# First rows of `a` by a broadcast transfer, block 0's carries ahead of the gate, and the last block's output in a tile for each sequence on two queues

## The chip, the cores and the metric

The kernel runs on one core of one Trainium2 chip. The metric is the device time of one execution in microseconds (us). Of repeated runs the median is quoted. A run is compared with runs of the kernel before on the same chip in the same rounds. On trace times: "at 23.67" is a time in us from the start of the profiled span, which is 1.7 to 1.8 us shorter than the device time.

## The reference

Two blocks in a row: a chunked state-space scan over 4 sequences of 768 steps with 8 heads, then an FFN over the 3072 tokens with a gate `h * cos(h)`. Cut to what matters:

```python
def _attn_ref(x, a, B, C):            # x (4,8,768,32), a (4,8,768), B and C (4,8,768,16)
    log_a = np.log(np.clip(a, 1e-06, 1.0))
    for c in range(nc):
        L = np.exp(cum[..., :, None] - cum[..., None, :]) * causal
        y[:, :, sl] = einsum(CB * L, xc) + einsum(Cc, state) * exp(cum)
        state = decay_full * state + sum(B_j x_j decay_from_j)

def _moe_ref(x, w_in, w_out):         # x (3072,256), w_in (256,2048), w_out (2048,256)
    h = x @ w_in
    return (h * np.cos(h)) @ w_out
```

The weights come as 8-byte floats and are turned into 4-byte ones on the chip, piece by piece.

## The kernel before

It works in 6 blocks of 128 steps for all 4 sequences (512 tokens). Block 0's scan runs alone; from then on, the FFN of block c (16 steps f: a product `hp`, a gate, a product `o`) is interleaved with the scan of block c + 1. TensorE carries nearly everything.

Block 0's decay rows: the row of each head has to stand in all 128 partitions. TensorE makes it by a product with a column of the identity, eight instructions for four heads:

```python
    def spread_a(b, tags):
        u, b_ = b // (NB // NU), b % (NB // NU)
        spread[b] = []
        for t in range(2):
            a_ps = bank([P, HH, P], "a_ps", tags[t])
            for h in range(HH):
                r = (b_ * H + t * HH + h) * NC
                PE.matmul(a_ps[:, h], lhsT=ident[0:RB, r:r + 1].to_broadcast([RB, P]),
                          rhs=cut[:, u], start=(h == 0), stop=True, skip_group_check=True)
            spread[b].append(a_ps)
```

A scan on the vector engine (DVE) turns each half into `lam`. Then transposes (`tp`), ScalarE's copies (`cT`, `bcT`), products `g`, DVE's `m`, products `y`, and the first FFN product. All transfers are issued by one queue, SyncE's (SP), in this order: `a`, then B, C, x of each sequence of block 0, six weight pieces, `a` back to DRAM, then for block 1:

```python
    load(1)                # B, C and x of all sequences, in pieces of 64, 64 and 128 bytes
    load_along(1)
    for b in range(NB):
        load_a(1, (b,))    # sequence b's decay rows, "arow"
        for n in (6 + 2 * b, 7 + 2 * b):
            fetch(*order[n])   # weight pieces
```

The main loop:

```python
    for n in range(NC * NF + LAG):
        c, f = divmod(n, NF)
        ...
            first(n)                                   # hp, k (ScalarE), w (DVE)
            if n + 3 < len(order):
                rest = grade(*order[n + 3], later=True)  # ScalarE, GpSimd: a weight piece
            if n + 2 < len(order):
                join(*order[n + 2])                    # DVE, GpSimd: the piece before it
            gate(n)                                    # sine (ScalarE), gT (DVE)
        if n >= LAG:
            second(n - LAG)                            # o
        if n < NB:
            carry(0, n)                                # s_ps (TensorE), state (DVE)
        if c + 1 < NC:
            ...   # (turn, intra, finish) of block c + 1: a sequence in three steps, from f = 3 on
```

At the end, four copies of `o` go into two output tiles, DVE and ScalarE in turn, and four transfers go out on SP's queue. In the last block `o` is a pair of PSUM tiles of two banks each, two sequences to a tile.

## Time and profile before

| | before |
|---|---|
| median of 3 runs | 410.0 us |
| TensorE busy, share of the span | 98% |
| first transpose | 9.22 us |
| first `hp` (f = 0) | 23.67 us |
| `hp` of f = 4 / f = 6 | 36.64 / 45.59 us |
| end of the last matmul / of the span | 404.2 / 408.6 us |

From the timeline of ScalarE: start, duration, engine, line, operation, operands, and in brackets the idle time in front of it and what ended it.

```profile
36.09 0.69 ACT L170 ACTIVATE mag<-words 128x512 f32<-128x512 f32 x1 [0.94 <-DMA words<-in_moe_w_in_dram]
```

ScalarE waits 0.94 us for a weight piece, the seventh asked for, in the middle of block 1's scan. TensorE waits for nothing there.

### The profile page before, as it was taken

How to read it: one execution, taken by the hardware profiler on the slowest of the kernel's cores; microseconds unless marked ns; L12 is line 12 of the kernel's file. 1: busy time of each engine (PE TensorE's matmuls, PEld its weight loads, DVE VectorE, ACT ScalarE, POOL GpSimd, SP SyncE). 2: the span in 40 equal slices, each digit the busy share in tenths (PEclk: the TensorE clock that was granted, in tenths of full speed). 3: DMA queues.
4: the chain of work that ended last, by engine and by line, in shares of the span. 5: the costliest groups of instructions: out<-in, count | busy, mean ns of one | idle time of the engine just before them, and what ended most of it. 6: DMA issues, size and time to landing. Idle time of an engine off the chain costs nothing.

```text
span 408.6 us, 5540 instructions
## 1 busy us (share of the span) xinstructions
PE 401.1 (98%) x2094; PEld 263.1 (64%) x2094; DVE 266.7 (65%) x410; ACT 173.8 (43%) x329; POOL 42.3 (10%) x62
## 2 busy tenths in 40 slices
PE   8999999999999999999999999999999999999995
PEld 6646666666666666666666666666666666666664
DVE  4989999945768754777663677674566664444442
ACT  2476666534343434344334433433434342433332
POOL 2164555400000000000000000000000000000000
PEclk9999999999999999999999999999999999999999
DMA  7999994291111092110164211120100000100001
GB/s 96 327 138 309 390 177 113 62 120 54 51 52 53 0 171 63 53 43 10 51 117 65 70 34 51 53 78 0 53 1 2 0 0 2 51 0 2 0 0 53
DMA packets 105979, 30.28 MB, mean 74 GB/s; under 512 B 75168, under 2 KB 101856, under 8 KB 105952
## 3 DMA queue, kind: packets, MB, share of 16 engines
q1 hardware_dynamic: 105952, 29.92, 30.9%
q8 instruction: 16, 0.26, 0.3%
q14 instruction: 11, 0.09, 0.1%
HBM read 26.57 MB, written 3.34 MB: 73 GB/s over the span
## 4 chain that ended last, share of the span: by engine, by line
PE 97%; ACT 1%; DVE 1%; issue 0%; DVEq 0%
PE hp L361 42%; PE o L385 41%; PE g L302 4%; PE y L324 3%; PE y L320 2%; PE a_ps L251 2%; PE warm L94 1%; PE tp L283 1%; PE tp L284 1%; PE s_ps L341 1%; PE y L94 0%; ACT cT L288 0%; ACT w L372 0%; DVE m L306 0%; DVE gT L374 0%
## 5 line engine op out<-in xcount | busy, mean ns | idle before, releaser
L361 PE MATMUL hp<-yT,w_in 128*128 128x512 f32 x384 | 185.0, 604 | 0.6 <-DVE gT L374 0.6
L385 PEld LDWEIGHTS o<-w_out,gT 128*128 128x128 f32 x768 | 145.9, 190 | 59.9 <-issue 44.0
L385 PE MATMUL o<-w_out,gT 128*128 128x256 f32 x768 | 181.1, 379 | 0.0
L365 ACT ACTIVATE k<-hp 128x512 int32<-128x512 f32 x96 | 57.4, 597 | 127.2 <-PE hp L361 127.1
L374 DVE TENSOR_TENSOR gT<-hp,w 128x512 f32<-128x512 f32 x96 | 66.3, 690 | 65.4 <-ACT w L372 65.4
L367 DVE SCALAR_TENSOR_TENSOR w<-hp,k 128x512 f32<-128x512 f32 x96 | 66.0, 687 | 62.3 <-ACT k L365 60.9
L361 PEld LDWEIGHTS hp<-yT,w_in 128*128 128x128 f32 x384 | 67.8, 190 | 57.7 <-issue 53.7
L372 ACT ACTIVATE w<-w,quarter 128x512 f32<-128x512 f32 x96 | 69.3, 722 | 75.1 <-DVE w L367 75.1
L267 DVE TENSOR_TENSOR_SCAN lam<-arow,unit 128x512 f32<-128x512 f32 x40 | 48.6, 1214 | 0.0
L306 DVE TENSOR_TENSOR m<-g,lam 128x512 f32<-128x512 f32 x48 | 30.7, 681 | 0.7 <-PE g L302 0.6
L276 POOL TENSOR_TENSOR sc<-bc,lam 128x128 f32<-128x128 f32 x20 | 8.2, 412 | 203.0 <-DVE lam L267 200.6
L288 ACT ACTIVATE cT<-tp,slot 128x128 f32<-128x128 f32 x48 | 14.6, 355 | 12.7 <-PE tp L284 12.7
L302 PE MATMUL g<-cT,bcT 32*128 32x256 f32 x192 | 17.1, 426 | 1.2 <-ACT bcT L290 1.2
L324 PE MATMUL y<-m,xr 128*32 128x128 f32 x384 | 15.8, 279 | 0.2 <-DVE m L306 0.2
L191 DVE SCALAR_TENSOR_TENSOR mag<-words,mag 128x512 uint32<-128x512 uint32 x16 | 13.4, 840 | 0.6
L329 ACT COPY yT<-y 128x256 f32<-128x256 f32 x24 | 8.9, 372 | 11.3 <-PE y L324 11.3
L302 PEld LDWEIGHTS g<-cT,bcT 32*128 32x128 f32 x192 | 7.5, 182 | 8.7 <-issue 6.5
L320 PEld LDWEIGHTS y<-bcT,state 128*128 128x128 f32 x80 | 12.1, 191 | 1.0
L171 POOL TENSOR_SCALAR mag<-mag 128x512 f32<-128x512 f32 x16 | 11.7, 731 | 9.4 <-ACT mag L170 9.2
L320 PE MATMUL y<-bcT,state 128*128 128x128 f32 x80 | 12.2, 274 | 0.0
L324 PEld LDWEIGHTS y<-m,xr 128*32 128x32 f32 x384 | 8.9, 109 | 4.3 <-DVE m L306 1.4
L170 ACT ACTIVATE mag<-words 128x512 f32<-128x512 f32 x16 | 10.9, 681 | 0.9 <-DMA words<-in_moe_w_in_dram 0.9
(43 smaller groups left out, 156.0 us busy)
## 6 DMA issues: line engine op xcount, KB each, us to landing
arow<-a_cut SPq DMA_DIRECT2D x20, 512.0 KB
words<-in_moe_w_in_dram SPq DMA_DIRECT2D x8, 512.0 KB
words<-in_moe_w_out_dram SPq DMA_DIRECT2D x8, 512.0 KB
xr<-in_x_dram SPq DMA_DIRECT2D x5, 512.0 KB
out_dram<-ob SPq DMA_DIRECT2D x10, 256.0 KB
bc<-in_B_dram SPq DMA_DIRECT2D x5, 256.0 KB
bc<-in_C_dram SPq DMA_DIRECT2D x5, 256.0 KB
along<-a_all SPq DMA_DIRECT2D x20, 64.0 KB
```

The source lines that it names most:

```text
L267: V.tensor_tensor_scan(out=lam[c, b][:, hs].rearrange("p h i -> p (h i)"), data0=rows_.rearrange("p h i -> p (h i)"), data1=unit.rearrange ...
L288: ACT.activation(cT[:, t], tp[:, 1], AF.Copy, scale=slot[:, t:t + 1])
L302: PE.matmul(g[u // 2][:, u % 2, 0:2 * P], lhsT=bcT[r, 0], rhs=cT[r].rearrange("p t i -> p (t i)"), start=True, stop=True)
L306: V.tensor_tensor(out=m[:, hs].rearrange("p (k t) i -> p k (t i)", k=2), in0=g[u][:, :, 0:2 * P], in1=l[:, hs].rearrange("p (k t) i -> p k ...
L320: PE.matmul(y[:, t], lhsT=s[:, t * P:(t + 1) * P], rhs=bcT[:, 1], start=(t == 0), stop=False, skip_group_check=True)
L324: PE.matmul(y[32 * q:32 * q + 32, t], lhsT=xr[:, b, h], rhs=m[:, h], start=(c == 0 and t == 0), stop=True, tile_position=(0, 32 * q), skip ...
L361: PE.matmul(hp[n], lhsT=w_in[:, k, f * P:(f + 1) * P], rhs=yT[c][:, k], start=(k == 0), stop=(k == KT - 1))
L365: ACT.activation(k, hp[n], AF.Copy, bias=0.25, scale=INV_2PI)
L367: V.scalar_tensor_tensor(out=w, in0=hp[n], scalar=INV_2PI, in1=k, op0=ALU.mult, op1=ALU.subtract)
L372: ACT.activation(cos, cos, AF.Sin, bias=quarter, scale=TWO_PI)
L374: V.tensor_tensor(out=gT[n], in0=hp.pop(n), in1=cos, op=ALU.mult)
L385: PE.matmul(o[c][b // 2][:, b % 2], lhsT=g[:, b * P:(b + 1) * P], rhs=w_out[:, f], start=(f == 0 and (last or b % 2 == 0)), stop=(f == NF ...
```

## The change

Three edits, each to shorten what TensorE or the end waits for: (1) sequence 0's first four heads get their rows by a broadcast transfer of 256 KB on ScalarE's queue, so that eight products fall away; (2) the states of block 0 are made ahead of the gates of n = 0, 1, 2, in DVE's idle time, instead of after the second product; (3) the last output gets a tile for each sequence, and two queues.

```diff
+    row0 = const.tile([P, HH, P], FP32, name="row0")
+    nc.scalar.dma_start(out=row0, in_=a[0, 0:HH, 0:P].unsqueeze(0).to_broadcast([P, HH, P]))
     a_in = const.tile([RB, NU, P], FP32, name="a_in")
 ...
+    V.tensor_scalar(out=row0, in0=row0, scalar1=1.0, scalar2=1e-6, op0=ALU.min, op1=ALU.max)
+    V.memset(row0[:, :, 0:1], 0.0)
 ...
-        spread[b] = []
-        for t in range(2):
+        spread[b] = [] if b else [row0]
+        for t in range(len(spread[b]), 2):
 ...
+        if last:
+            for b in range(NB):
+                ob = two.tile([P, DM], FP32, tag="ob1", bufs=NB, name="ob")
+                (ACT.copy if b == 1 else V.tensor_copy)(out=ob, in_=o[c][b // 2][:, b % 2])
+                (nc.scalar if b % 2 else nc.sync).dma_start(out=rows_[:, b, c, :], in_=ob)
+            return
 ...
+            for b in ((0,), (1, 2), (3,))[n] if n < 3 else ():
+                carry(0, b)
             gate(n)
 ...
-        if n < NB:
-            carry(0, n)
```

More of the change, by code (lines that the diff above doesn't have):

```diff
@@ L390, in second @@
         rows_ = out.rearrange("(b c p) m -> p b c m", b=NB, p=P)
-        count = 1 if last else 2
-        for i in range(0, NB, count):
-            if i % 2 == 0:
-                ob = two.tile([P, 2, DM], FP32, tag="ob", name="ob")
-            bs = slice(i % 2, i % 2 + count)
-            (ACT.copy if (i // count) % 2 else V.tensor_copy)(out=ob[:, bs],
-                                                             in_=o[c][i // 2][:, bs])
-            nc.sync.dma_start(out=rows_[:, i:i + count, c, :], in_=ob[:, bs])
+        if last:
[4 more added lines that the diff above has]
+            return
+        for i in range(2):
+            ob = two.tile([P, 2, DM], FP32, tag="ob", name="ob")
+            (ACT.copy if i else V.tensor_copy)(out=ob, in_=o[c][i])
+            nc.sync.dma_start(out=rows_[:, 2 * i:2 * i + 2, c, :], in_=ob)
     fill(bank([P, 4, P], "warm", "o"), 2)
-    spread_a(0, ("h", "h"))
+    spread_a(0, (None, "h"))
     decays(0, 0, 0)
```

## The prediction

> **What bounds the kernel now.** I read the page first, then the chain that ended last in order of time, then the timeline of the first 33 us and of the last 6 us, since the change touches only these two stretches.
>
> ```profile
> PE 401.1 (98%) x2094; PEld 263.1 (64%) x2094; DVE 266.7 (65%) x410; ACT 173.8 (43%) x329; POOL 42.3 (10%) x62
> ...
> PE 97%; ACT 1%; DVE 1%; issue 0%; DVEq 0%
> ```
>
> TensorE carries 97% of the chain. Between 36 and 403 us nothing of the program changes, so what can be won is time before the first FFN products find their rhythm, and time after the last matmul. The chain, in order of time, shows the beginning:
>
> ```profile
> 1.12 3.78 PE warm L94 x4
> 4.90 4.48 PE a_ps L251 x32
> 9.39 0.11 PE tp L283
> 9.50 0.12 PE tp L284
> 9.62 0.02 issue
> 9.64 0.63 ACT cT L288 x2
> ...
> 27.77 0.70 DVE gT L374
> 28.48 0.14 issue
> 28.61 1.96 PE hp L361 x4
> 30.57 1.73 PE o L385 x8
> 32.29 0.25 PE s_ps L341 x8
> ```
>
> Columns: start, duration, engine, tile, line. To see: 32 a_ps matmuls stand between the warm-up fills and sequence 0's transposes, on TensorE itself; and from 25.64 to 28.61 the chain leaves TensorE (k, w, sine, gT), because the third hp waits for gT to free one of two hp banks. TensorE's wait there is 0.57 us on the timeline ("PE hp L361 <- DVE gT L374: 0.6, 1").
>
> DVE's timeline of the same place:
>
> ```profile
> 26.29 0.69 DVE L367 SCALAR_TENSOR_TENSOR w<-hp,k 128x512 f32<-128x512 f32 x1
> 27.77 0.69 DVE L374 TENSOR_TENSOR gT<-hp,w 128x512 f32<-128x512 f32 x1 [0.79 <-ACT w L372]
> 28.38 0.41 DVE L346 TENSOR_TENSOR state<-s_ps,own 128x256 f32<-128x256 f32 x1
> 28.82 0.69 DVE L367 SCALAR_TENSOR_TENSOR w<-hp,k 128x512 f32<-128x512 f32 x1
> 29.43 0.42 DVE L189 TENSOR_SCALAR mag<-mag 128x512 uint32<-128x512 uint32 x1
> 29.88 0.98 DVE L191 SCALAR_TENSOR_TENSOR mag<-words,mag 128x512 uint32<-128x512 uint32 x1
> 30.78 0.68 DVE L374 TENSOR_TENSOR gT<-hp,w 128x512 f32<-128x512 f32 x1
> ```
>
> DVE has one hole, 0.79 us before gT(0); after it it is full until about 52 us. The end:
>
> ```profile
> 403.35 0.42 DVE L396 COPY ob<-o 128x256 f32<-128x256 f32 x1 [1.46 <-PE o L385]
> 403.80 1.83 SPq L398 DMA_DIRECT2D out_dram<-ob  x4
> 403.81 0.37 ACT L396 COPY ob<-o 128x256 f32<-128x256 f32 x1 [2.64 <-DVE ob L396]
> 404.21 0.42 DVE L396 COPY ob<-o 128x256 f32<-128x256 f32 x1 [0.44 <-PE o L385]
> 404.67 0.37 ACT L396 COPY ob<-o 128x256 f32<-128x256 f32 x1 [0.49 <-DVE ob L396]
> ```
>
> Two copies share a tile, so ACT's copy follows DVE's although it needs other columns. Both DVE copies start only when a pair of sequences is through on TensorE (403.33 and 404.19).
>
> **What the Trainium skill says.** "TensorE: Matmul & The Clock Gate", section "What's actually happening": TensorE starts at half rate, and the warm-up is an amount of busy time, not of matmuls. The trace agrees in kind: the first nine a_ps matmuls start 0.213 us apart, from 6.77 us on they start 0.111 us apart. (It says some 3.4 us; here the fast rate comes 5.5 us after the first fill, and the measurement decides.) So leaving out the first eight a_ps matmuls does not save eight slow ones. "DMA: Bandwidth & Descriptors", section "Issuing engines are not separate DMA queues": DMAs started from different engines run on the same 16 DMA engines and interleave; a second queue saves only issue time. No other issuing queue is in use before, so this trace cannot show it; it does show the 16 engines full from 3 us on (busy share 0.95 to 1.05 in most 2 us stretches from 4 to 24). The same page, "Anatomy of one DMA", gives a fixed cost near 2 us for a DMA from GpSimd, mostly completion. Here, from Sync, a_in issues at 0.81 and lands at 2.58 to 2.95; the last output issues at 405.22 and lands at 407.00 on fifteen engines and at 407.54 on one.
>
> **Part 1, first rows by broadcast.** Removed: the 8 a_ps matmuls of heads 0 to 3. Added: a 256 KB transfer (512 pieces of 512 B) on ACT's queue, a DVE clip over 128x512 (0.42 us, as L189 takes) and a small memset (0.06 us, as the one on quarter). TensorE still starts a_ps at 4.70, after the fills. Eight slow steps end at 6.405 as before, then two of 0.213 and 0.148, then 14 of 0.111: 6.405 + 0.36 + 1.56 = 8.33 against 9.22 for the first transpose: **0.89 us** earlier, 8 x 0.111. On DVE the first scan can run before 6.65 and three instead of four follow it: 1.11 us earlier. The smaller counts, as m(0,0) also needs g from TensorE (it started at 11.23, g ended at 11.19). From there to hp(0) at 23.71 the chain is TensorE, ACT and DVE in turn with nothing that is fixed in time, so hp(0) moves to 22.8.
>
> Is row0 there in time? Its scan must start by 5.5, its clip by 5.0. a_in's pieces of 512 B take 27 ns each; 512 of them on 16 engines are 0.86 us, doubled by interleaving with the B and C pieces: landing near 4 us (an estimate). There is a microsecond left. The 0.86 us push later loads: the first weight piece lands at 14.05, now near 14.9; ACT takes it at 14.35 and has 1.67 us of idle time after it, so this costs nothing. a_in itself may come 0.4 us later; cut was ready at 3.87 and TensorE was in its fills until 4.70.
>
> **Part 2, carries ahead of the gate.** state(0) takes 0.41 us; it moves into DVE's hole before gT(0) and costs nothing. Carry 2 (0.25 us on TensorE) moves from behind o(0) into TensorE's wait before hp(2): **0.25 us** won. But carry 3 now stands behind hp(2) and ahead of o(0). The carries' banks come from a pair in rotation, so carry 3 takes the bank of carry 1, which is free after state(1); and DVE reaches state(1) only after w(1) and the join (L189, L191). In the shifted clock: k(1) ends on ACT at 27.9 (28.79 - 0.89), w(1) to 28.6, L189 to 29.0, L191 to 29.95, state(1) to 30.3. TensorE ends hp(2) at 28.61 - 0.89 + 1.96 = 29.68 and waits until 30.35: **0.67 us lost**. Then 0.25 (carry 3), 1.73, 1.91, 1.73 and 0.37 (tp) give hp(4) at 36.34 against 36.80: 0.46 us are left of the 0.89 + 0.25. The DVE delay before gT(1) (state 1 and 2 first: to 31.3) is hidden, as hp(3) cannot start before 32.3.
>
> **Part 3, the end.** Copies b0 and b1 start together at 403.35. b2 starts at 404.21 as before, b3 follows it on DVE: done near 405.06 against 405.04, no gain. Only the issue changes: before, Sync issued b3 at 405.22, being busy with b2 until 405.17; ACT's free queue does it at about 405.09. **0.13 us**. The tail of 2.3 us from issue to landing remains.
>
> Sum: 0.89 + 0.25 - 0.67 + 0.13 = 0.60 us of 410.0: **409.4 us**.
>
> **Rivals.**
> (a) No wait at carry 3, as L191 runs in 0.69 us as elsewhere, or state(1) comes sooner: up to 0.67 us more, 408.7. For it: L191 took 0.69 in other places. Against: a Pool instruction ran beside it both times that it took 0.98 here, and that neighbour shifts along.
> (b) The early gain is eaten by block 1's first row transfer. arow for block 1, sequence 0 lands at 34.57 and its scan starts at 35.37, on a DVE that has no idle time. With 0.5 to 0.8 us more DMA work ahead it lands at 35.1 to 35.4, while DVE now gets to that scan at about 34.9. DVE then keeps little of its lead here; but state(3), 0.41 us at 39.00, is out of its way, and m(1,0) ended at 44.65 with y's second half needing it at 45.2. So TensorE can be earlier by some 0.9 before it waits. If ACT also waits for a weight piece (it did for 0.94 us at 36.09), the gain falls to 0.2: 409.8.
> (c) row0 arrives after 5 us, delayed in the crowd of 64 B pieces: the second scan is late by as much and part 1 gives 0 to 0.5: 409.6 to 410.2. Against: only 2000 pieces move before 4 us, and the queues alternate.
> (d) The tail. One DMA engine served the last outputs a microsecond late, behind an instruction fetch at 405.38. If that fetch falls elsewhere, 0.5 us more is won; if it stays, part 3 wins nothing.
>
> **Range and chances.** The sum of the parts runs from about 0 (b or c) to 1.7 (a and d). The three times before span 0.9 us, which is as large as the effect. I take 408.4 to 410.2. 2% are 8.2 us, far beyond every rival: within 2% has 0.98.
>
> **What would show it.** Part 1: the first scan reads row0 before 5.5 us, the first transpose is at about 8.3, hp(0) at 22.8. If the first scan starts later than 5.5, (c) holds. Part 2: state(0) before gT(0); a TensorE wait of about 0.7 us at s_ps for DVE's state between hp(2) and o(0); none would make it (a). hp(4) at 36.3; at y of block 1 a new wait for m would be (b). Part 3: two copies at 403.35 less the shift, an ACT issue, the last landing 0.1 us closer to the last matmul. The prediction is wrong if the distance from hp(4) to the last matmul changes by more than 0.3 us, since nothing there is said to change.

## The result, and the profile after

Whole change: 410.72 us (409.81 to 411.93, 6 runs) against 409.9 (409.17 to 410.71, 6 runs). Ratio 1.002, 95% interval 1.0001 to 1.0039. The change did not gain 0.6 us; it lost 0.8. The time lies above the range (410.2).

The page's line of the chain that ended last, by engine, after:

```profile
PE 92%; SPq 4%; DMA 1%; ACT 1%; DVE 0%; issue 0%; DVEq 0%; ACTq 0%
```

Before, 97% was TensorE and no transfer stood in it. Now the SP queue and a transfer do. The chain in order of time (start, duration, what):

```profile
4.91 3.23 PE a_ps L256 x24
8.13 0.11 PE tp L288
...
17.25 7.01 SPq L112
...
31.64 5.79 DMA words<-in_moe_w_in_dram
...
38.10 0.66 ACT w L377
...
39.29 0.60 ACT cT L293 x2
39.90 0.16 ACT bcT L295
...
40.10 1.03 PE g L307 x7
```

The first two lines show part 1 at work: 24 products instead of 32, and the first transpose at 8.13 instead of 9.39 in this view. Then the chain runs over SP's queue, one issue of which lasts 7 us, to a weight piece that lands at 37.43, and from there over ScalarE, which works through its instructions in order (the piece, the sine, `cT`, `bcT`), to TensorE's `g` of block 1. The sine's input was there at 36.78 (DVE's `w`), but the sine stands behind the piece and starts at 38.10. The timeline has the waits themselves:

```profile
26.52 0.69 DVE L379 TENSOR_TENSOR gT<-hp,w 128x512 f32<-128x512 f32 x1 [0.46 <-ACT w L377]
...
30.01 0.32 PE L346 MATMUL s_ps<-xr,sc 128*32 128x64 f32 x8 [0.70 <-DVE state L351]
...
34.97 1.23 DVE L272 TENSOR_TENSOR_SCAN lam<-arow,unit 128x512 f32<-128x512 f32 x1 [0.76 <-DMA arow<-a_cut]
...
37.51 0.69 ACT L173 ACTIVATE mag<-words 128x512 f32<-128x512 f32 x1 [2.85 <-DMA words<-in_moe_w_in_dram]
38.84 0.69 DVE L379 TENSOR_TENSOR gT<-hp,w 128x512 f32<-128x512 f32 x1 [1.01 <-ACT w L377]
40.10 1.03 PE L307 MATMUL g<-cT,bcT 32*128 32x256 f32 x8 [0.74 <-ACT bcT L295]
```

DVE's hole before gT(0) is smaller (0.46 instead of 0.79), as state(0) now stands in it. TensorE waits 0.70 us at carry 3 for DVE's state. DVE waits 0.76 us for the first rows of block 1, which it did not before. ScalarE waits 2.85 us for the seventh weight piece instead of 0.94, and passes that on to DVE and TensorE. The end:

```profile
403.77 0.42 DVE L399 COPY ob<-o 128x256 f32<-128x256 f32 x1 [1.46 <-PE o L390]
...
404.23 0.37 ACT L399 COPY ob<-o 128x256 f32<-128x256 f32 x1 [2.64 <-DVE ob L399]
404.63 1.13 ACTq L400 DMA_DIRECT2D out_dram<-ob  x2
404.63 0.76 DVE L399 COPY ob<-o 128x256 f32<-128x256 f32 x2 [0.44 <-PE o L390]
```

ScalarE's copy waits for DVE's just as before, although the output tiles are now separate.

Where TensorE's lead went, by the start of `hp` in the two traces:

| start of | before | after | difference |
|---|---|---|---|
| first transpose | 9.22 | 7.97 | -1.25 |
| f = 0 | 23.67 | 22.41 | -1.26 |
| f = 2 | 28.61 | 27.36 | -1.25 |
| f = 3 | 32.47 | 32.09 | -0.38 |
| f = 4 | 36.64 | 35.75 | -0.89 |
| f = 5 | 40.82 | 41.06 | +0.24 |
| f = 6 | 45.59 | 46.01 | +0.42 |
| f = 16 (block 1) | 87.30 | 87.72 | +0.42 |
| end of the last matmul | 404.18 | 404.59 | +0.41 |

Between f = 4 and f = 6, 1.31 us are lost, and after that nothing moves any more. From f = 0 to f = 4, 0.37 us are lost (13.34 us instead of 12.97): that is part 2.

### The profile page after: what moved, and what is told of

Same layout as the page of the kernel before. It is cut to its first block, busy times and chain, and to the rows that moved or that the text cites. A ratio compares the mean times of both kernels' runs of the same rounds, so it can differ in the third digit from the quotient of the medians.

```text
span 408.7 us, 5526 instructions
## 1 busy us (share of the span) xinstructions
PE 400.2 (98%) x2086; PEld 262.1 (64%) x2086; DVE 267.1 (65%) x413; ACT 173.3 (42%) x328; POOL 42.7 (10%) x62
## 4 chain that ended last, share of the span: by engine, by line
PE 92%; SPq 4%; DMA 1%; ACT 1%; DVE 0%; issue 0%; DVEq 0%; ACTq 0%
PE hp L366 40%; PE o L390 39%; PE g L307 4%; PE y L329 3%; SPq L112 2%; PE y L325 2%; PE a_ps L256 2%; DMA words<-in_moe_w_in_dram 1%; SPq L129 1%; PE warm L94 1%; PE tp L289 1%; PE tp L288 1%; ACT cT L293 0%; PE s_ps L346 0%; DVE lam L272 0%
## 5 line engine op out<-in xcount | busy, mean ns | idle before, releaser
L293 ACT ACTIVATE cT<-tp,slot 128x128 f32<-128x128 f32 x48 | 14.6, 356 | 9.3 <-PE tp L289 9.3
```

Source lines behind the costliest of these rows:

```text
L293: ACT.activation(cT[:, t], tp[:, 1], AF.Copy, scale=slot[:, t:t + 1])
```

## The experiments

The theory after this reading ("late weights"): the 256 KB stand ahead of everything that the same 16 DMA engines have to bring, all later transfers come later, and their arrival sets the time of f = 6, whatever lead TensorE has. The first rival ("carry stall"): the 0.70 us at carry 3 are the loss. A second ("unlucky profile"): arrivals scatter from run to run, and the broadcast has nothing to do with it.

### The three parts alone, and the whole change with one transfer moved

`p1_rows_alone`, `p2_carries_alone` and `p3_end_alone` have one part of the diff each. `whole_x_late` is the whole change with the cut below (`load` gets an option that leaves x out and returns a function that issues it):

```diff
-    load(1)
+    x_later = load(1, late=True)      # B and C only
     load_along(1)
     for b in range(NB):
         load_a(1, (b,))
         for n in (6 + 2 * b, 7 + 2 * b):
             fetch(*order[n])
+        if b == 0:
+            x_later()                 # block 1's x, 512 KB in pieces of 128 bytes
```

Expected of part 1 alone:

> Part 1 alone (first rows by broadcast), the carries and the end as before. Theory (late weights): the first FFN product starts about 1.2 us earlier than in the kernel before, but the 256 KB put ahead of everything make block 1's first row transfer and the seventh weight piece land 0.8 to 1.4 us later; ScalarE waits for that piece 2 us or more instead of 0.94, and the lead is gone at the first product of block 1's second sequence (f = 6, before 45.59 us): there -0.2 to +0.5. Ratio 0.999 to 1.001. Rival (carry stall): what ate the lead in the whole change was the 0.70 us wait of TensorE at carry 3; without it part 1 keeps 0.9 us or more, ratio about 0.9975.

Measured: 410.56 us against 409.84, ratio 1.001 (0.9998 to 1.0022). The rows of block 1 and the seventh piece landed 1.2 us later than before, ScalarE waited 2.6 us for the piece, and f = 6 came 0.38 us later, as expected. A miss: the first `hp` came only 0.5 us earlier (23.17) instead of 1.2, as ScalarE waited 2.9 us for the first weight piece. Of part 2 alone:

> Part 2 alone (carries ahead of the gate). Both theories: TensorE waits 0.6 to 0.7 us at carry 3 for DVE's state and wins 0.25 at carry 2. Theory (late weights): the arrivals are those of the kernel before, so the seventh piece lands near 36.0 and what is lost at carry 3 stays visible: hp of f = 4 0.1 to 0.4 us later, ratio 1.000 to 1.001. Rival (carry stall costs the whole): ratio 1.002.

Measured: 410.66 us, ratio 1.0005 (0.999 to 1.002). TensorE waits 0.7 us at carry 3, as in the whole change. From f = 0 to f = 4 it took 13.35 us, 0.38 more than before. `hp` of f = 4 came 0.3 us earlier all the same, not later as expected, since the first transpose came at 8.42 instead of 9.22. And the seventh piece came at 37.44 instead of near 36.0, without any broadcast: a miss of the theory, and the first sign that arrivals scatter. Of part 3 alone:

> Part 3 alone (a tile for each sequence, two queues). ScalarE's copy of sequence 1 still waits for DVE's copy of sequence 0, as in the whole change, so that wait did not come from the shared output tile. From the last matmul's end to the span's end: 4.1 us against 4.4 before, so 0.3 us faster, ratio 0.999 to 1.000; everything before the last matmul as in the kernel before within 0.2 us.

Measured: 409.68 us, ratio 0.9988 (0.9975 to 1.0001). ScalarE's copy waited for DVE's, and from the last matmul to the end it took 3.6 us, 0.5 less than expected. Of the whole change with x late:

> The whole change, but block 1's x (512 KB in 128 B pieces, some 3.3 us of all DMA engines, first needed near 44 us) is issued after the first row transfer and the seventh and eighth weight piece of block 1 instead of before them. Theory (late weights): those pieces land some 3 us earlier, ScalarE's wait for weights there goes below 0.3 us and DVE's wait for the rows to nothing, and the lead of hp of f = 4 (0.9 us) is kept at f = 6: 0.8 to 1.3 us faster than the whole change, ratio to before 0.997 to 0.999. Rival (carry stall): arrivals don't matter, no change against the whole change, ratio 1.002.

Measured: 409.37 us, ratio 0.9984 (0.9971 to 0.9996). `hp` of f = 4 at 35.48 and of f = 6 at 44.43: nothing is lost between them. ScalarE's wait for weight pieces is not below 0.3 us (0.9), a miss, but it no longer holds up TensorE. From the table of TensorE's waits in that run:

```profile
PE s_ps L348 <- DVE state L353: 0.7, 1, 0.7
PE hp L368 <- DVE gT L381: 0.5, 1, 0.5
```

The wait at carry 3 is as long as in the whole change, and yet the kernel is faster than before. The carry stall as the whole cause falls. (The columns are the us in total, how often, and the longest.)

### Is it the reorder alone, and is it the 256 KB?

`before_x_late` is the kernel before with the reorder above and nothing else. `broadcast_unused` is the kernel before with the first two added lines of the diff (the transfer into `row0`), never read.

> The kernel before with only block 1's x issued later (none of the three parts). Separates the reorder's own worth from what it lets the change keep. Theory (the early lead is real, the arrivals cap it): in the kernel before, the arrivals are just in time (ScalarE waits 0.94 us for the seventh piece, TensorE nowhere), so the reorder alone is worth at most 0.3 us; hp of f = 6 between 45.2 and 45.7; ratio 0.999 to 1.000. Rival (the reorder alone makes the 1.3 us seen with the whole change): hp of f = 6 near 44.5, ratio 0.9975 or less.

Measured: 410.14 us against 410.58, ratio 0.9988 (0.9976 to 1.0). f = 4 at 36.24, f = 6 at 45.20. The reorder alone gave 0.44 us by the medians, a little more than expected. In its profile the seventh piece lands at 34.82, 1.2 us earlier than before; the profile of `before_again` below shows that the kernel before has late arrivals too.

> The kernel before with only the 256 KB broadcast added, loaded and never read. Theory (these bytes push every later arrival): the first row transfer and the seventh weight piece of block 1 land 0.7 to 1.0 us later than in the kernel before, hp of f = 4 stays within 0.2 us of it, hp of f = 6 comes 0.3 to 0.6 us later; ratio 1.0005 to 1.0015. Rival (arrivals scatter by a microsecond from run to run whatever the bytes; in the run of part 2 alone, which has no such transfer, the piece was as late): no difference that the interval can show, ratio 0.9995 to 1.0005.

Measured: 411.48 us, ratio 1.0027 (1.0008 to 1.0046): more than expected. The direction is the theory's, and the unused transfer costs. Its profile, which is that of the slowest of its six runs (412.99), has the seventh piece 3.6 us later, far more than the expected 0.7 to 1.0, and shows a second place: the first weight piece landed at 17.75 (14.05 before), and `hp` of f = 0 came at 25.29 instead of 23.67. So f = 4 did not stay within 0.2 us, a miss: the prediction's and the theory's belief that the first piece had room enough was wrong as well.

### Carry 3, and the PSUM tiles at the end

`x_late_carry3_behind` adds to `whole_x_late`:

```diff
-            for b in ((0,), (1, 2), (3,))[n] if n < 3 else ():
+            for b in ((0,), (1, 2))[n] if n < 2 else ():
                 carry(0, b)
 ...
             second(n - LAG)
+        if n == 2:
+            carry(0, 3)
```

> The whole change with x late, and carry 3 issued behind the second product of n = 2 instead of ahead of its gate. State 1 is then done before TensorE comes to carry 3: the 0.7 us wait at s_ps vanishes, hp of f = 3 comes 0.6 to 0.8 us earlier than with x late alone. If nothing else binds in block 1, that stays: 0.5 to 0.8 us faster than with x late alone, ratio to before 0.996 to 0.9975. Rival (the wait was hidden: the next limit, DVE's row scan or ScalarE's queue, caps f = 6 at the same time): ratio as with x late alone, 0.998 to 0.999.

Measured: 409.75 us against 410.58, ratio 0.998 (0.9968 to 0.9992). The wait at `s_ps` is gone: from `hp` of f = 2 to f = 3 it takes 3.86 us (27.93 to 31.79) instead of 4.75 with x late alone (27.07 to 31.82). From f = 0 to f = 4 it took 12.57 us, less than the 12.97 of the kernel before. In time nothing is seen of it; in this profile the seventh piece came at 36.34 and f = 6 followed f = 4 after 9.36 us instead of 8.95. The rival was right on the ratio. `x_late_carry3_o_tiles` adds, for the last block:

```diff
-            o[c] = [pair("o")[:, :, 0:DM] if last else bank([P, 2, DM], "o", "o")
-                    for _ in range(2)]
+            if last:
+                o[c] = ([pair("o")[:, 0, 0:DM] for _ in range(2)] +
+                        [bank([P, DM], "o", "o") for _ in range(2)])
 ...
-                (ACT.copy if b == 1 else V.tensor_copy)(out=ob, in_=o[c][b // 2][:, b % 2])
+                (ACT.copy if b % 2 else V.tensor_copy)(out=ob, in_=o[c][b])
```

> As the run with carry 3 behind, and the last block's four PSUM sums in four tiles of a bank each, ScalarE copying sequences 1 and 3. Theory: what tied ScalarE's copy to DVE's was the shared PSUM tile, not the output tile; now each copy starts when its own sequence's last matmul ends, the last copy ends 0.4 us after the last matmul instead of 0.8, and the time from the last matmul to the end falls by 0.3 to 0.5 us: ratio 0.0008 to 0.0012 below the run with carry 3 behind. Rival (instruction order, not tiles): the copy still waits for DVE and nothing changes.

Measured: 409.31 us, ratio 0.9969 (0.9957 to 0.9981), 0.0011 below the run before it in the same rounds, though the intervals overlap. The timeline settles the cause:

```profile
402.10 0.37 ACT L406 COPY ob<-o 128x256 f32<-128x256 f32 x1 [2.18 <-PE o L397]
...
402.53 0.42 DVE L406 COPY ob<-o 128x256 f32<-128x256 f32 x1 [0.44 <-PE o L397]
402.96 0.37 ACT L406 COPY ob<-o 128x256 f32<-128x256 f32 x1 [0.49 <-PE o L397]
```

Both of ScalarE's copies are now released by TensorE and not by DVE, and the last ends at 403.33, 0.4 us after the last matmul (402.93). In this kernel two engines that read one PSUM tile were put one after the other; separate output tiles didn't change that. From the last matmul to the span's end it takes 3.96 us against 4.10 in the run before it: less than the 0.4 us that the copies gained. That distance lies between 3.63 and 4.46 us over all profiles, so a single one says little. One late share of the last output makes most of this scatter (see rival (d) below); without it the distance fell from 3.59 to 3.20, by all of the 0.4 us.

### The same kernels again, and part 1 with nothing in its way

> The kernel before once more, unchanged: a second profile and a control of the comparison itself. Ratio 1.000 with an interval that holds 1. The seventh weight piece lands between 35.9 and 37.5 us (the profiles with this order of transfers had 36.01, 36.24 and, with part 2 alone, 37.44); the first transpose between 8.4 and 9.4 us, by when the fast TensorE clock comes. hp of f = 6 between 45.4 and 46.3.

Measured: 410.58 us against 410.58, ratio 0.9992 (0.997 to 1.0014). The piece came at 37.08, `hp` of f = 6 at 46.03: the kernel before has such runs too.

> The whole change once more, unchanged. Theory (the 256 KB push all later transfers by 0.7 to 1.0 us, and their arrival sets block 1): sequence 0's x lands at 6.0 to 6.6 again (5.3 to 5.7 without the transfer), the seventh piece at 37.0 or later, TensorE waits 0.7 us at carry 3, and hp of f = 6 comes at 45.8 to 46.8 whatever the first transpose's time; ratio 1.000 to 1.003. Rival (the first profile was an unlucky one): the piece lands before 36.5, hp of f = 6 before 45.2, ratio 0.998 or less.

Measured: 412.06 us against 410.58, ratio 1.0028 (1.0003 to 1.0053). x of sequence 0 at 6.13, the piece at 37.96, the wait at carry 3 0.7 us, f = 6 at 46.52, although f = 4 was at 36.42. The second profile repeats the first; the "unlucky profile" falls for the whole change.

`best_without_rows` has x late, carries 0 to 2 ahead of the gate and carry 3 behind, and the four PSUM tiles, but no part 1. `best_with_rows` is `x_late_carry3_o_tiles` again.

> x late, carries 0 to 2 ahead of the gate and carry 3 behind the second product, four PSUM tiles at the end, but without part 1: no broadcast, sequence 0's rows from TensorE as before. Theory (with the arrivals out of the way, part 1 earns its 8 products of 0.111 us): 0.5 to 0.9 us slower than the same kernel with part 1 in this job. Rival (the pushed arrivals cost as much as part 1 earns): same within 0.3 us, and the seventh piece lands 0.7 us earlier.

> The run with x late, carry 3 behind and four PSUM tiles once more, in the same job as the one without part 1. Ratio 0.996 to 0.998 again, hp of f = 6 at 43.9 to 44.9; last copy 0.4 us after the last matmul.

Measured: 409.42 us without (0.996, 0.9936 to 0.9984) and 408.87 with rows (0.9953, 0.9931 to 0.9975), against 410.58. By the means of their six runs they differ by 0.27 us, inside the scatter; expected were 0.5 to 0.9. With rows, f = 6 came at 45.36, later than the expected 43.9 to 44.9, and the ratio was better than expected: two misses. In the profile with rows the first transpose came 1.5 us earlier (7.53 against 9.03), and the first `hp` at the same 23.48. ScalarE's timeline of that run shows why:

```profile
15.97 0.69 ACT L175 ACTIVATE mag<-words 128x512 f32<-128x512 f32 x1 [3.17 <-DMA words<-in_moe_w_in_dram]
```

It sits 3.17 us in front of the first weight piece, which landed at 15.95, with the copies of sequence 2 behind it in its queue. So two more runs, with that piece asked for ahead of the fourth sequence's loads, with and without the broadcast:

```diff
         for b in range(NB if each else 1):
 ...
+            if each and b == NB - 1:
+                fetch(*order[0])
 ...
-    for n in (0, 2, 1, 3, 4, 5):
+    for n in (2, 1, 3, 4, 5):
```

> The best version with rows, and the first weight piece asked for ahead of the fourth sequence's B, C and x (its transposes come at 16.5 us or later). Theory (ScalarE's wait for that piece is what takes part 1's lead inside block 0): the piece lands before 13.8 us, ScalarE waits less than 0.6 us for it, from the first transpose to the first FFN product 14.4 to 14.6 us as in the kernel before (14.45), and the first product comes at 21.7 to 22.6; ratio 0.993 to 0.9955. Rival (the fourth sequence's loads, now later, bind in its place): TensorE or ScalarE waits for B or C of sequence 3, the distance stays over 15 us, ratio 0.996 or more.

> The same without the broadcast. Theory (part 1 earns 8 products of 0.111 us once nothing late binds): 0.5 to 1.0 us slower than the same kernel with rows in this job, ratio 0.995 to 0.9975. Rival (part 1 is worth nothing, the broadcast costs what it saves): within 0.3 us of it.

Measured: 409.07 us (0.9974, 0.9961 to 0.9988) with rows and 409.24 (0.9977, 0.9962 to 0.9992) without, against 410.16. In block 0 the theory holds: with rows the piece lands at 13.30, ScalarE waits 0.70 us for it (0.1 over what was expected), the way from the first transpose to the first `hp` is again 14.45 us, and `hp` of f = 0 is at 21.81, f = 4 at 34.37, 2.2 us ahead of the run without. But in time part 1 shows no more than 0.2 us here either, inside the scatter: f = 5 comes at 39.48 and f = 6 at 44.82, only 0.7 us ahead of the run without rows (45.49). The lead is taken by the next arrivals instead: the seventh piece, at 35.87, makes TensorE wait 0.5 us at `g`, and the first rows of block 1, at 34.61, hold up DVE and through it TensorE at `y`:

```profile
34.64 1.22 DVE L276 TENSOR_TENSOR_SCAN lam<-arow,unit 128x512 f32<-128x512 f32 x1 [1.02 <-DMA arow<-a_cut]
...
43.49 0.71 PE L329 MATMUL y<-bcT,state 128*128 128x128 f32 x4 [0.31 <-DVE m L315]
```

Both ratios missed what was expected of them.

### What all profiles say together

The piece's landing is the last of its 16 shares, as the trace has them.

| run | seventh piece lands | `hp` f = 4 | `hp` f = 6 | f = 6 less f = 4 | f = 6 less landing |
|---|---|---|---|---|---|
| before | 36.01 | 36.64 | 45.59 | 8.95 | 9.58 |
| part 3 alone | 36.24 | 36.74 | 45.70 | 8.96 | 9.46 |
| before, x late | 34.82 | 36.24 | 45.20 | 8.96 | 10.38 |
| whole, x late | 33.82 | 35.48 | 44.43 | 8.95 | 10.61 |
| best without rows | 35.31 | 36.05 | 45.00 | 8.95 | 9.69 |
| x late, carry 3 behind, PSUM tiles | 34.80 | 35.22 | 44.22 | 9.00 | 9.42 |
| first piece early, no rows | 35.76 | 36.54 | 45.49 | 8.95 | 9.73 |
| before, again | 37.08 | 35.98 | 46.03 | 10.05 | 8.95 |
| part 2 alone | 37.44 | 36.33 | 46.20 | 9.87 | 8.76 |
| part 1 alone | 37.20 | 36.14 | 45.97 | 9.83 | 8.77 |
| whole | 37.43 | 35.75 | 46.01 | 10.26 | 8.58 |
| whole, again | 37.96 | 36.42 | 46.52 | 10.10 | 8.56 |
| broadcast unused | 39.65 | 38.25 | 48.41 | 10.16 | 8.76 |
| x late, carry 3 behind | 36.34 | 35.56 | 44.92 | 9.36 | 8.58 |
| best with rows | 36.77 | 36.05 | 45.36 | 9.31 | 8.59 |
| first piece early | 35.87 | 34.37 | 44.82 | 10.45 | 8.95 |

In the upper seven, f = 6 follows f = 4 after 8.95 to 9.00 us: TensorE's own work. In the lower nine it comes later than that, 8.6 to 8.95 us after the piece's landing.

The table alone doesn't show that it is always this piece. The first rows of block 1 (`arow`) are asked for just ahead of it on the same queue and land 1.3 to 2.8 us before it, and in seven of the nine DVE waits 0.8 to 1.2 us for them. In the chains of "before, again" and "first piece early" the rows stand in the piece's place, and f = 6 comes 10.29 and 10.21 us after they land. So late arrivals set f = 6; which of the two binds changes from run to run. The reorder moves both, and no run separates them.

Block 0 has the same form: the first `hp` comes 14.4 to 14.6 us after the first transpose, or 7.53 us after the first weight piece, whichever is later (part 1 alone: 15.64 + 7.53 = 23.17, as measured; best with rows: 15.95 + 7.53 = 23.48, as measured).

What the broadcast does to arrivals: x of sequence 0 lands at 5.25 to 5.76 us in the profiles without it and at 6.09 to 6.53 in those with it. The ranges don't touch. The seventh piece, with the original order, lands at 36.01, 36.24, 37.08 and 37.44 without (mean 36.7) and at 37.20, 37.43, 37.96 and 39.65 with it (mean 38.1). So the push is real, and a scatter of more than a microsecond lies over it. (Without the profile of the unused broadcast, that of a slow run, the second mean is 37.5.)

## Why the prediction was wrong

**Part 1, on TensorE: right; that more came was the clock.** 0.89 us were predicted, 1.25 came in the first pair of profiles. The prediction took it that the fast clock comes at the same time in both. But the `a_ps` products start at the fast rate from 6.77 us on before and from 5.96 on after. With steps of 0.213 and 0.111 us, each microsecond of slow clock costs about 0.48 us: 0.81 x 0.48 = 0.39, which with the 0.89 makes the 1.25 to within 0.03. Over eight profiles with and eight without the rows, the first transpose came at 7.25 to 8.63 (mean 7.80) and at 8.42 to 9.52 (mean 9.04), a difference of 1.24, and the fast rate from 4.57 to 7.40 (mean 5.63) and from 5.07 to 7.40 (mean 6.36). Take off 0.48 us for each microsecond before the fast rate, and every profile has the first transpose within 0.1 us of its group's mean, and the groups 0.89 us apart: the predicted size. The rest is when the fast clock came, which scatters by more than the two means differ. `row0` came in time (its scan started at 4.86, limit 5.5), so rival (c) fell.

**Part 1, the step that failed: "this costs nothing".** The prediction had the push right (0.86 us worked out; x of sequence 0 came 0.8 later). It then looked at one transfer, the first weight piece, compared one landing with one moment at which ScalarE took it, and gave ScalarE's idle time as room. For that piece in this pair it was right: the first `hp` came 14.44 us after the first transpose, as before (14.45). What cost were the next ones, block 1's first rows and the seventh piece, which the sum left out and which stood in a rival only: from f = 4 to f = 6 it took 10.26 us instead of 8.95. In the original order this distance was 9.83 to 10.26 in all four profiles with the broadcast, and 10.05 and 9.87 in two of the four without, so scatter alone can do it, but not each time. Two things were missing. The lead itself eats the room: everything that waits moves up while the transfer moves back. And a landing in one profile isn't a fixed time: the first piece came at 14.05 to 15.45 in the runs with the original loads of block 0 and no broadcast, and up to 17.75 with it. In four of the runs with rows or with the unused broadcast it held up the first `hp` by 0.5 us or more.

**Rival (b) came true, and was too small.** It named the rows and the weight piece of block 1 and gave the kernel 0.2 us of gain in the worst case. It argued that DVE had slack before `y`. But in the first profile the limit is ScalarE, which works in order: the sine of f = 3 and the copies of block 1's first sequence stand behind the late piece, so `g` was late as well as `m`. Of the lead of 0.89 us at f = 4 nothing was left and 0.42 more was lost. The prediction's own test ("the distance from hp(4) to the last matmul changes by more than 0.3 us") says so: it was 367.54 us and became 368.84.

**Part 2: right.** TensorE's wait at carry 3 was 0.70 us, predicted 0.67, and it vanished when carry 3 was moved. What part 2 keeps, predicted at a loss of 0.42 us, can't be told in the time: alone it measured 1.0005 with an interval of 0.15% to either side. On TensorE the traces show it: from f = 0 to f = 4 it took 12.97 us before, 13.34 after (0.37 lost), and 12.57 with carry 3 behind (0.40 won).

**Part 3: the term right and low, a reading beside it wrong.** The last issue came 0.82 us after the last matmul instead of 1.04, on ScalarE's free queue as predicted: 0.22 us where 0.13 were predicted. The copies b0 and b1 were to start together. They did not, as they share a PSUM tile; this had no part in the sum, and the last copy ended about 0.8 us after the last matmul, as before. Alone the part measured 0.9988, 0.16 us by the medians, with an interval that reaches 1.0001, so the time by itself does not show the gain.

**Rival (d)**, the instruction fetch in the tail, can be followed in the landings. In fifteen of the sixteen profiles one of the last output's 16 shares lands 0.24 to 0.81 us after the others. In part 3 alone it was 0.03 us: there the fetch began 2.24 us after the last matmul (0.6 to 1.8 in the others), and the tail was the shortest, 3.63 us, as the rival has it. Without this share the tail is 3.8 to 3.9 us with the old end, 3.6 with part 3 and 3.2 to 3.3 with the four PSUM tiles. That it is the fetch that makes the share late fits, but was not tested.

**Left open.** Why the arrivals scatter by over a microsecond with the same order of transfers. In the first profile after, one DMA engine fetched 16 KB of instructions from 31.0 us on for 1.34 us, and the last two shares of the seventh piece landed at 36.97 and 37.43, the others by 36.51. That fits, but was not tested. Which of block 1's two arrivals, rows or seventh piece, would have to move. And whether part 1 can earn its 0.89 us at all: it would need both weight pieces and the rows out of the way at once, and moving one let another bind.

The best version is the whole change with x late, carry 3 behind the second product and four PSUM tiles: 0.9953 in one set of rounds and 0.9969 in another, against 1.002 and 1.0028 for the change as it was. Without the broadcast the same version gave 0.996, so most of that does not come from part 1.

## What to carry to other kernels

When a stage is fed just in time, moving its start ahead gains nothing until the feed moves too: before counting a lead, list every transfer that the next stages wait for and compare its landing with the new time of need, over several runs. Bytes added in front of a full queue move the transfers behind them, so order transfers by when they are needed; here moving one 512 KB load back gave 0.9988 alone, and taking eight products off the critical engine 1.001 alone (each with an interval that reaches 1). And look at the in-order engine behind a late transfer: what stands behind it is late too, though its own inputs are there.

## What the Trainium skill lacked or had wrong

- "DMA: Bandwidth & Descriptors", section "Issuing engines are not separate DMA queues": that transfers of different queues share the engines agrees with the run with the unused broadcast on ScalarE's queue (x of sequence 0, on SP's queue, at 6.53 instead of 5.28 us). It says that the issue time is "usually small relative to the DMA itself", and gives no measure of when it isn't. Block 1's C, 4096 pieces of 64 bytes behind other transfers, held SP's queue for 7.01 us in its issue alone (7.08 before, of 10.67 us from issue to landing), and the issues behind it waited that long.
- "TensorE: Matmul & The Clock Gate", section "What's actually happening": the slow start is given as some 3.4 us, with a change that varies by 500 ns to either side from run to run. The variation is there and is larger: in the trace before, the products start at the fast rate from 5.65 us after the first matmul on, and over all sixteen from 3.5 us or less to 6.3 us after it. It matters at this scale: in the eight profiles without the rows the first transpose came between 8.42 and 9.52 us.
- No page says what instruction fetches cost other transfers (it would belong to "Runtime: NRT & Kernel Launch", section "Instruction fetch mechanics"). The traces list them among the packets of the DMA engines: 16 KB took 0.9 to 1.4 us in the trace before and up to 2.4 us in the others. At the end of the kernel before an 8 KB fetch began at 405.38, and one share of the last output landed at 407.54, the other fifteen by 407.00; that the one made the other late is not shown.
- "PSUM — Partial Sum Buffer", section "PSUM bank collisions raise a hardware error", asks for order between engines in one bank. No page says that readers of one tile can be put in order though they read different banks of it: here ScalarE's copy started 0.46 us after DVE's (404.23 against 403.77), when that had ended, and tiles of their own removed that wait.
